# A second dense half, pairwise transposes of x, earlier weight loads and an explicit token order in an attention and MLP kernel

## The chip, the cores and the metric

The kernel runs on one core of one Trainium2 chip. The metric is the device time of one execution in microseconds (us). A timed execution is a little longer than the profiled span of the same run: 338.30 us beside a span of 336.5 us for the changed kernel. "x2", "y1" and the like are short names of experiments, which are told below. Where several executions were timed, medians are given. A ratio is the mean time of one kernel's fast runs over that of the other's fast runs of the same rounds, so it is not quite the ratio of the medians quoted. "Fast", "slow" and "unknown" are the states that each run was recorded with; a single look has the state "unknown".

## The reference

Block-sparse attention feeds a two-layer MLP with an exact GELU. Four batches, eight heads, 768 positions, 64 channels; blocks of 32 positions, so 24 blocks.

```python
mask = abs(blk_i - blk_j) <= 1
mask |= (blk_i == 0) | (blk_j == 0) | (blk_i == 23) | (blk_j == 23)
for qb in range(24):                        # three drawn key blocks for each query block
    for kb in sampled_blocks[qb]:
        mask[qb*32:qb*32+32, kb*32:kb*32+32] = True
attn = softmax(where(mask, q @ k.T / 8, -1e9)) @ v
x    = attn.transpose(0, 2, 1, 3).reshape(3072, 512)
out  = gelu(x @ w_in) @ w_out               # w_in 512 x 2048, w_out 2048 x 512
```

The first and the last block row attend to all keys. The text calls these the "dense rows".

## The kernel before

The work is cut into eight halves of 384 rows (two per batch), and a half goes through attention, the hidden layer and the output layer. The kernel overlaps the MLP of one half with the attention of the next. So a run has nine stages, which I bound by the first `hp` (hidden-layer) matmul of each half: an opening (attention of the first half alone), seven stages with the MLP of one half and the attention of the next, and a last one with an MLP alone.

Sparse attention gathers key blocks into `kg` and value blocks into `v_gat` with indirect copies on POOL. The first half of batch 0 instead computes all scores, with a one-hot matmul that adds -30000 to the barred blocks, and so needs no gathers:

```python
def first_scores(hp, t):                    # dense scores of a pair of heads, key tile t
    for l, r_, first_ in ((onehot..., barred..., True), (st["k", hp], st["q", hp], False)):
        for h in range(2): pe.matmul(s1[:, h, 0:HALF], lhsT=l[r, c], rhs=r_[r, 0:HALF], ...)
    act.activation(first_pt[hp % 3][:, t], s1[:, :, 0:HALF], AF.Exp, scale=scale)
```

A "record" is one DMA transfer as the profile lists it; the profile's views call it a packet. v goes through the queue of SP (sync). k, q and the weights go through the queue of POOL (gpsimd), but for the first k and q, which SP loads ahead of v. The weights wait until v has been cast: `after_values` touches w_in's tile on DVE after the casts, and the load must follow that write.

```python
first_v = load_v(0, sp)          # 6 loads of 256 KB, each record 64 floats = 256 B
...
for w in "kq": st["st", w, 1] = load_qk(0, w, 1)      # POOL's queue, records of 768 B written
...
def after_values():
    for n in range(NT): own_v(0, first_v, n, n + 1, dve)      # v_flat <- st_v, six casts
    for c in range(2):
        dve.memset(w_in_sb[:, 0:1, 1024 * c:1024 * c + 1], 0.0)
        load_w_in(c)                                   # POOL's queue
extra = {..., (2, 1): after_values and value_validity,
         (3, 1): first_weighted(1), load_w_out(0), load_w_out(1), four gathers of k, ...}
```

The other parts that the argument touches:

```python
mm_pool = tc.tile_pool(name="mm_pool", bufs=2, space=PSUM)  # op, psx, psd and ps share 2 buffers

def transpose_qk(b, hp, which, pair, eng, st):
    dst = qkt_pool.tile([P, S], BF16, tag=f"t{which}", ...)   # tk or tq
    ps = mm_pool.tile([P, NT, P], BF16, tag="mm", name="ps")
    ... 12 pe.transpose ...
    cast(eng, dst..., ps...)                                  # on DVE

def transpose_x(b, hb, m, st):          # after all four pairs: rows m of x, four transposes
    ps = mm_pool.tile([P, KIN, P], BF16, tag="mm", name="psx")
    ...
def place_xd(b, hb, st):                # dense rows into xT, just before the hidden layer
    dve.tensor_copy(st["xT", hb][:, :, c], st["xdT"][:, :, hb*BLOCK:hb*BLOCK+BLOCK])
```

The order of issue came from two helpers: `weave` put a given number of output steps between attention steps, and `spread` put the gathers and transposes for later evenly among the hidden steps.

The softmax here doesn't subtract the row's maximum and nothing guards it: scores larger than these inputs give would overflow.

Of the kernel before, what the change touches and what calls it, by code (L numbers as in the profile page):

```python
# [58 lines left out]
def weave(main, fill):  # L59

    fill = list(fill)
    for step, n in main:
        step()
        for f in fill[:n]:
            f()
        del fill[:n]
    for f in fill:
        f()


def spread(steps, aux):

    out, n, m = [], len(steps), len(aux)
    for i, step in enumerate(steps):
        out += aux[m * i // n:m * (i + 1) // n] + [step]
    return out
# [3 lines left out]
def kernel(  # L80
# [23 lines left out]
    kg_pool = ctx.enter_context(tc.tile_pool(name="kg_pool", bufs=4))  # L104
# [3 lines left out]
    first_ctx = ExitStack()  # L108
    first = first_ctx.enter_context(tc.tile_pool(name="first", bufs=1))
# [27 lines left out]

    sts = [dict() for _ in range(B)]
# [4 lines left out]
    for i, (w, x) in enumerate((("k", k), ("q", q))):  # L143
        t = w_out_sb.bitcast(F32)[:, 3 * i:3 * i + 3, :].rearrange("p a c -> p (a c)")
        first_st[w] = t.rearrange("p (h c) -> p h c", h=2)
        sp.dma_start(out=first_st[w], in_=x[0, 0:2].rearrange("h (p j) d -> p h (j d)", j=NT))
        if i == 0:
            sp.dma_start(out=raw,
                         in_=bass.AP(tensor=src, offset=0, ap=[[0, P], [1, NB * NR * 2]]))
# [31 lines left out]

    key_i = small("key_i", [1], I32)
    key_b = small("key_b", [1])
    onehot = small("onehot", [NB, BLOCK], BF16, first)
    seen = small("seen", [NB // 2])
# [3 lines left out]
    dve.tensor_scalar(onehot, blocks.unsqueeze(2).to_broadcast([P, NB, BLOCK]),  # L189
                      key_b[:, 0:1], None, op0=ALU.is_equal)  # L190
    dve.tensor_scalar(seen, blocks[:, 0:NB // 2], key_b[:, 0:1], None, op0=ALU.subtract)
# [5 lines left out]
    dve.memset(seen[:, 0:1], 1.0)  # L197

# [8 lines left out]
    for t in kgl[0] + qgl:  # L207
        dve.memset(t, 0.0)
    dve.memset(v_own[0][:, :, :, D:2 * GW], 1.0)

    sbi = small("sbi", [NB, NR], I32)
    sbf = small("sbf", [NB, NR])
    hit = small("hit", [NB // 2, NR])
    barred = small("barred", [NB // 2, BLOCK], BF16, first)
    dve.tensor_copy(sbi, raw[:, :, :, 0])
    dve.tensor_copy(sbf, sbi)
    dve.tensor_scalar(hit, sbf[:, 0:NB // 2, :], key_b[:, 0:1], None, op0=ALU.is_equal)
    for s in range(NR):
        dve.tensor_add(seen, seen, hit[:, :, s])
    dve.tensor_scalar(barred, seen.unsqueeze(2).to_broadcast([P, NB // 2, BLOCK]),  # L220
# [15 lines left out]
    iota(mask_ka, [[4, 4], [1, NR]], 0, 0)  # L236
    iota(rowm, [[4, 4]], 3, 0)
    iota(cols, [[4, 3]], 3, 0)
    iota(qbt, [[1, NQ], [0, NR]], 1, 0)
    pool.memset(base_v, float(NULL))  # L240
    iota(base_v[96:128, 3::4], [[1, 5]], 0, 0)
    iota(base_v[96:128, 2:19:4], [[1, 5]], 7, 0)
# [3 lines left out]
    for w in "kq":  # L246
        st["st", w, 1] = load_qk(0, w, 1)

# [165 lines left out]
    def gather_k(b, hb, hp, st):  # L414
        kg = kg_pool.tile([P, NQH, P], BF16, tag=f"kg{hb}", name=f"kg{hb}")
        st["kg", hb, hp] = kg
        pool.indirect_copy(
            kg.bitcast(F32).rearrange("p n (s c) -> p (n s) c", c=BLOCK // 2),
            st["k", hp].bitcast(F32).rearrange("p (n c) -> p n c", c=BLOCK // 2),
            idx_k[:, hb, 0:3], i_know_this_is_slow=True)  # L420


    def scores(b, hb, hp, st):
# [3 lines left out]
        pt = p_pool.tile([P, 2, 2, 512], BF16, tag="pt", name="pt")  # L427
# [44 lines left out]
    def weighted(b, hb, hp, st):  # L472
        pt, vo, gl = st["pt", hb, hp], v_own[b % 2], vgl[b % 2]
        x = st["x", hb]
# [18 lines left out]
        normalise(x[:, :, hp * P:hp * P + P].rearrange("p m (h d) -> p m h d", h=2), og, MH)  # L493
# [11 lines left out]
    first_pt = [first.tile([P, NT, 2, HALF], BF16, name="first_pt")]  # L505
    for t in v_gat:
        first_pt.append(t.rearrange("p n h e -> p (n h e)")[:, 0:NT * 2 * HALF]
                        .rearrange("p (t h c) -> p t h c", t=NT, h=2))

    def first_scores(hp, t):  # L510
        s1 = sc_pool.tile([P, 2, 512], F32, tag="sc", name="s1")
        c = slice(t * P, t * P + P)
        for l, r_, first_ in ((onehot.rearrange("p n c -> p (n c)"),
                               barred.rearrange("p n c -> p (n c)"), True),
                              (st["k", hp], st["q", hp], False)):
            for h in range(2):
                r = slice(64 * h, 64 * h + 64)
                pe.matmul(s1[:, h, 0:HALF], lhsT=l[r, c], rhs=r_[r, 0:HALF],
                          start=first_, stop=not first_)
        act.activation(first_pt[hp % 3][:, t], s1[:, :, 0:HALF], AF.Exp, scale=scale)  # L520

    def first_weighted(hp):
        og = og_pool.tile([P, MH, 2, VW], F32, tag="og", name="og")
        for m in range(MH):
            for h in range(2):
                for t in range(NT):
                    pe.matmul(og[:, m, h, :], lhsT=first_pt[hp % 3][:, t, h, m * P:m * P + P],
                              rhs=v_own[0][:, t, 2 * hp + h, 0:VW],
                              start=(m == h == t == 0), stop=True, skip_group_check=True)
        normalise(st["x", 0][:, :, hp * P:hp * P + P].rearrange("p m (h d) -> p m h d", h=2),  # L530
                  og, MH)

    def new_x(b, hb, st):
        st["x", hb] = x_pool.tile([P, MH, D_MODEL], BF16, tag="x", name="x")
        st["xT", hb] = x_pool.tile([P, KIN, HALF], BF16, tag="xT", name="xT")
        if hb == (b == 0):
            st["xd"] = x_pool.tile([P, NPAIR, P], BF16, tag="xd", name="xd")

    def transpose_x(b, hb, m, st):
        x, xT = st["x", hb], st["xT", hb]  # L540
        ps = mm_pool.tile([P, KIN, P], BF16, tag="mm", name="psx")
        for i in range(KIN):
            pe.transpose(ps[:, i, :], x[:, m, i * P:i * P + P], ident)
        lo, hi = (BLOCK if b > 0 and hb == m == 0 else 0), (P - BLOCK if hb == 1 and m == MH - 1 else P)
        dve.tensor_copy(xT[:, :, m * P + lo:m * P + hi], ps[:, :, lo:hi])
# [13 lines left out]

    def attention_steps(b, hb, st):  # L560

        new_x(b, hb, st)
        S_ = lambda hp: lambda: scores(b, hb, hp, st)
        W_ = lambda hp: lambda: weighted(b, hb, hp, st)
        D_ = lambda hp: lambda: dense_scores(hp, st)
        E_ = lambda hp: lambda: dense_weighted(b, hp, st)
        X_ = lambda m: lambda: transpose_x(b, hb, m, st)
        if hb == (b == 0):
            steps = [(S_(0), 3), (D_(0), 2)]
            for hp in range(1, NPAIR):  # L570
                steps += [(S_(hp), 0), (E_(hp - 1), 0), (W_(hp - 1), 2), (D_(hp), 2)]
            steps += [(E_(3), 0), (W_(3), 3), (lambda: transpose_xd(st), 0),
                      (X_(0), 0), (X_(1), 1), (X_(2), 0), (lambda: place_xd(b, hb, st), 0)]
        else:
            steps = [(S_(0), 5)]
            for hp in range(1, NPAIR):
                steps += [(S_(hp), 0), (W_(hp - 1), 4)]
            steps += [(W_(3), 3), (X_(0), 0), (X_(1), 1), (X_(2), 0),
                      (lambda: place_xd(b, hb, st), 0)]
        return steps  # L580

# [46 lines left out]
    def first_pair(hp):  # L628
        i = 2 * (hp % 2)
        for w in "kq":  # L630
            pair = st["st", w, hp // 2][:, i:i + 2, :]
# [3 lines left out]
        for w in "kq":  # L635
            globals_qk(0, hp, w, pool, st)

    def load_batch(b):
        st = sts[b]
        for n in range(2):  # L640
            for w in "kq":
                st["st", w, n] = load_qk(b, w, n)


    def after_values():
        for n in range(NT):
            own_v(0, first_v, n, n + 1, dve)
        for c in range(2):
            dve.memset(w_in_sb[:, 0:1, 1024 * c:1024 * c + 1], 0.0)
            load_w_in(c)  # L650

    def rotate_first():
        for r in range(1, 4):
            dve.memset(v_all[:, NT * r:NT * r + 1, 0:1, 0:1], 0.0)
            rotate_v(0, r, sp)

    new_x(0, 0, st)
    first_pair(0)
    extra = {(0, 3): lambda: first_pair(1),
             (1, 1): lambda: first_pair(2),  # L660
             (1, 3): lambda: first_pair(3),
             (2, 1): lambda: [after_values(), value_validity()],
             (2, 3): lambda: [first_weighted(0), gather_constants(), key_indices()],
             (3, 1): lambda: [first_weighted(1), load_w_out(0), load_w_out(1)]
             + [f() for f in k_steps(0, 1, range(NPAIR))],
             (3, 3): lambda: [first_weighted(2), rotate_first(), value_columns()]}
    for hp in range(NPAIR):
        for t in range(NT):
            first_scores(hp, t)
            extra.get((hp, t), lambda: None)()  # L670
    first_weighted(NPAIR - 1)
    for m in range(MH):
        transpose_x(0, 0, m, st)
    value_indices(0, dve)
    clear_mask()
    for i in range(2):
        clear_globals(i, dve)
    for i in range(2):
        mark_valid(i)
    first_ctx.close()  # L680
    g_pool = ctx.enter_context(tc.tile_pool(name="g_pool", bufs=1))
    os_pool = ctx.enter_context(tc.tile_pool(name="os_pool", bufs=2))

    value_indices(1, dve)
    sts[1]["st", "v"] = load_v(1, sp, dve)

    def transpose_step(b, hp):
        i = 2 * (hp % 2)
# [96 lines left out]
```

## Time and profile before

| | before |
|---|---|
| timed | 322.62 us (321.71 to 323.01, 4 runs) |
| span of the profiled run | 320.1 us |
| PE busy | 273.6 us, 85% |
| stages, us | 37.6, 44.1, 44.7, 32.2, 37.6, 32.2, 36.6, 30.4, 24.9 |
| v's last record begins | 19.8 us |
| w_in's load may begin | after the casts of v, which end at 23.0 us |

The prediction below read two boundaries by eye, 37.5 and 29.6; by one rule they are 36.6 and 30.4, with the same sum.

The page of the kernel before, its first two parts. The digits are tenths of busy share in 40 equal slices of 8 us; PEclk is the granted clock of the tensor engine in tenths.

```profile
span 320.1 us, 8104 instructions
PE 273.6 (85%) x3560; PEld 163.4 (51%) x3560; DVE 136.8 (43%) x366; ACT 156.1 (49%) x206; POOL 100.7 (31%) x149
...
PE   1778596698993998989997998989997989899995
...
PEclk9999899799996899999999999999999999999999
DMA  6949999999960049007791590009500000010001
```

PE is full from the middle on, so PE is what a change must relieve. The first third has holes, and the clock drops to 7, 6 and 8 there. The waits of PE in the same kernel (engine and tile, who released it; then us in total, number, longest) name the holes.

```profile
PE ps L54 <- ACT st L54: 7.7, 2, 4.8
PE s L54 <- POOL kg L54: 5.7, 2, 5.1
PE op L54 <- DMA w_out_sb<-in_moe_w_out_dram: 5.1, 2, 3.1
```

The first is the start of the kernel, the longest part of the second (5.1 us, up to 101.2 us, in stage 3) waits for the key gathers of batch 1, which stand on POOL behind that batch's value gathers (these from 88.71 us on, the first key gather from 99.95 to 101.14), and the third for w_out, which comes late because it stands behind the gate (POOL issues w_in at 23.3 us and w_out at 24.8).

From 51 to 57 us the second batch's v (q1, 256 B records) shared the DMA engines with w_out (q0, 1024 B records). The DMA view of that window gives packets, MB and a share of the engines:

```profile
q0 software_dynamic: 930, 0.94, 91.6%
q1 hardware_dynamic: 925, 0.24, 29.7%
```

The two queues moved the same number of records, and so very different numbers of bytes.

### The profile page before, as it was taken

To read this page: it belongs to the slowest core of one execution; us is meant where nothing else is said; L and a number is where in the kernel's file an instruction comes from. 1 tells how busy PE (TensorE), PEld (TensorE's weight loads), DVE (VectorE), ACT (ScalarE), POOL (GpSimd) and SP (SyncE) were. 2 spreads that over 40 slices of the span, in tenths; PEclk is the share of its full clock that TensorE was granted. 3 is DMA by queue.
4 is the path that set the end of the run, shared out by engine and by line. 5 is a ranking of instruction groups with operands and counts; after the bars stand their busy time and mean duration, and the time that the engine had idled before them with its cause. 6 is when DMAs were issued, how large, how long until landed. Compare 5 with 4: busy or idle time off the path is not lost. (4 is left out here: it accounts for less than half of the span.)

```text
span 320.1 us, 8104 instructions
## 1 busy us (share of the span) xinstructions
PE 273.6 (85%) x3560; PEld 163.4 (51%) x3560; DVE 136.8 (43%) x366; ACT 156.1 (49%) x206; POOL 100.7 (31%) x149
## 2 busy tenths in 40 slices
PE   1778596698993998989997998989997989899995
PEld 0345353464561654646564654646564645465642
DVE  5488871066460355415632555245440461035001
ACT  3587066254343660466256651576247634753620
POOL 6133422610054554343445554321244430000000
PEclk9999899799996899999999999999999999999999
DMA  6949999999960049007791590009500000010001
GB/s 156 205 94 167 216 234 199 191 209 237 250 132 0 20 76 173 35 0 175 198 202 29 69 199 33 2 2 240 167 2 2 35 35 33 2 35 35 33 35 66
DMA packets 42131, 33.79 MB, mean 106 GB/s; under 512 B 26096, under 2 KB 36464, under 8 KB 42096
## 3 DMA queue, kind: packets, MB, share of 16 engines
q1 hardware_dynamic: 31024, 23.18, 29.3%
q0 software_dynamic: 11072, 10.09, 20.2%
q8 instruction: 28, 0.46, 0.6%
q14 instruction: 7, 0.06, 0.1%
HBM read 27.34 MB, written 6.29 MB: 105 GB/s over the span
## 5 line engine op out<-in xcount | busy, mean ns | idle before, releaser
L54 PE MATMUL op<-w_out_sb,g 128*128 128x512 bf16 x384 | 97.3, 390 | 5.1 <-DMA w_out_sb<-in_moe_w_out_dram 5.1
L54 ACT ACTIVATE g<-hp 128x768 bf16<-128x768 f32 x64 | 51.7, 810 | 85.5 <-PE hp L54 85.5
L54 PE MATMUL hp<-xT,w_in_sb 128*128 128x384 bf16 x512 | 88.4, 331 | 1.9 <-DVE os L54 0.9
L54 PEld LDWEIGHTS <-w_in_sb 128*128 128x128 bf16 x512 | 49.5, 99 | 36.9 <-issue 4.4
L54 ACT ACTIVATE pt<-s 128x1024 bf16<-128x1024 f32 (+2 forms) x84 | 51.6, 687 | 26.1 <-PE s L54 13.3
L54 DVE TENSOR_TENSOR pt<-pt,mask_x 128x768 bf16<-128x768 bf16 x28 | 17.4, 620 | 96.6 <-ACT pt L54 96.4
L54 POOL INDIRECT_COPY v_gat<-v_flat,idx_v 128x1024 f32 (+1 forms) x21 | 33.4, 1592 | 78.4 <-issue 36.6
L54 POOL INDIRECT_COPY kg<-tk,idx_k 128x704 f32 x28 | 34.1, 1219 | 67.8 <-issue 58.1
L54 PEld LDWEIGHTS <-g 128*128 128x128 bf16 x384 | 34.5, 100 | 38.5 <-issue 8.3
L54 DVE COPY tk<-ps 128x768 bf16<-128x768 bf16 x16 | 15.3, 957 | 33.2 <-PE ps L54 33.2
L54 ACT ACT_TABLE_LOAD x16 | 20.5, 1283 | 17.9 <-PE s L54 9.3
L54 DVE COPY os<-op 128x512 f32<-128x512 f32 x24 | 16.6, 692 | 24.2 <-PE op L54 22.2
L54 PEld LDWEIGHTS <-tk 64*128 64x128 bf16 (+1 forms) x312 | 15.1, 98 | 20.2 <-issue 16.7
L54 PE MATMUL ps<-ident,st 128*64 128x128 bf16 x384 | 15.0, 229 | 8.0 <-ACT st L54 7.7
L54 PE MATMUL s<-tq,kg 64*128 64x32 bf16 x616 | 12.3, 174 | 10.8 <-POOL kg L54 5.7
L54 PEld LDWEIGHTS <-pt 128*32 128x32 bf16 (+1 forms) x868 | 19.8, 97 | 2.5 <-DVE x L54 0.3
L54 PE MATMUL s<-tq,tk 64*128 64x128 bf16 (+1 forms) x216 | 18.5, 252 | 1.3 <-ACT pt L54 0.7
L54 PEld LDWEIGHTS <-st 128*64 128x64 bf16 x384 | 12.0, 114 | 13.4 <-ACT st L54 7.9
L54 DVE TENSOR_TENSOR x<-og,rc 128x384 bf16<-128x384 f32 x32 | 17.8, 558 | 1.1
L54 ACT ACTIVATE pd<-sd 128x768 bf16<-128x768 f32 x16 | 13.0, 813 | 9.9 <-PE sd L54 9.9
L54 PEld LDWEIGHTS <-kg 64*128 64x128 bf16 x616 | 11.2, 94 | 12.5 <-issue 6.3
L54 PE MATMUL psx<-ident,x 128*128 128x128 bf16 x96 | 9.3, 219 | 9.0 <-DVE xT L54 3.7
(110 smaller groups left out, 233.2 us busy)
## 6 DMA issues: line engine op xcount, KB each, us to landing
st_v<-in_v_dram SPq DMA_DIRECT2D x24, 256.0 KB, 6.1
out_dram<-os SPq DMA_DIRECT2D x24, 256.0 KB, 3.1
v_flat<-v_flat SPq DMA_DIRECT2D x8, 594.0 KB, 7.3
v_flat<-v_flat SPq DMA_DIRECT2D x8, 396.0 KB, 5.5
st<-in_k_dram POOLq DMA_DIRECT2D x7, 384.0 KB, 7.2
st<-in_q_dram POOLq DMA_DIRECT2D x7, 384.0 KB, 10.3
w_in_sb<-in_moe_w_in_dram POOLq DMA_DIRECT2D x2, 1024.0 KB, 13.1
w_out_sb<-in_moe_w_out_dram POOLq DMA_DIRECT2D x2, 1024.0 KB, 32.3
```

The costliest lines, as they stand in the source:

```text
L54: return self._tc.keep_in_program_order(f(*args, **kwargs))
```

## The change

The intent: (a) let the second half of batch 0 attend densely too, so that batch 0 needs no gathers and no rotation of its v; (b) transpose x pair by pair, as soon as a pair is normalised; (c) replace the two ordering helpers by strings of tokens, one for each phase, which say exactly what is issued when; and (d) issue the weights' loads at once, without the gate. The core of the diff, cuts marked by "...":

```diff
-def weave(main, fill): ...
-def spread(steps, aux): ...
+OPENING = """
+A0 P0 P1 F00 F01 F02 F03 A1 F04 F05 F10 F11 F12 A2 F13 F14 F15 J0 J1 J2 J3 J4 J5 F20 F21 V0 F22 A3 F23 X0 F24 F25
+F30 V1 F31 F32 X1 F33 V2 F34 F35 X2 V3 X3 N L1"""
+FIRST = """
+H I0 H I1 H M1 I2 H H I3 H I4 H I5 H
+O2 F00 F01 O2 F02 F03 O2 F04 F05 O1 I6 F10 F11 V0 F12 F13 X0 O2 I7 F14 F15 O2 F20 F21 V1 F22 F23 B R X1 O2 I8
+F24 F25 T0 K00 O2 F30 F31 V2 F32 F33 X2 O2 T1 K01 F34 F35 O2 V3 Q0 Q1 O2 X3 O3"""
+SECOND = """
+H H T2 K02 C00 C01 C02 H H T3 K03 G H H H M2 H
+..."""
+SPARSE = """
+H H H H H H H H
+O2 S0 O6 B R W0 S1 O3 X0 T0 K00 W1 S2 O3 X1 T1 K01 W2 S3 O4 X2 C00 C01 C02 W3 O4 X3 Z O2"""
+...
     for w in "kq":
         st["st", w, 1] = load_qk(0, w, 1)
+    for c in range(2):
+        load_w_in(c)
...
-    def first_scores(hp, t):
+    def first_scores(hb, hp, t):
...
-    def transpose_x(b, hb, m, st):
-        x, xT = st["x", hb], st["xT", hb]
-        ps = mm_pool.tile([P, KIN, P], BF16, tag="mm", name="psx")
-        for i in range(KIN):
-            pe.transpose(ps[:, i, :], x[:, m, i * P:i * P + P], ident)
+    def transpose_x(b, hb, hp, st):
+        x, xT = st["x", hb, hp], st["xT", hb]
+        ps = og_pool.tile([P, MH, P], BF16, tag="og", name="psx")
+        for m in range(MH):
+            pe.transpose(ps[:, m, :], x[:, m, :], ident)
...
-    def after_values():
-        for n in range(NT):
-            own_v(0, first_v, n, n + 1, dve)
-        for c in range(2):
-            dve.memset(w_in_sb[:, 0:1, 1024 * c:1024 * c + 1], 0.0)
-            load_w_in(c)
-
-    def rotate_first(): ...
```

The tokens that the text uses: H is two tiles of the hidden layer, O2 two output steps, F dense scores, V a dense weighted sum, J a cast of v, T the transposes of k and q of a pair, K and C gathers of keys and values, X a transpose of x, Z the placing of dense rows, P the load of half of w_out, L1 the loads of k and q of batch 1.

## The prediction

> **What bounds it now.** The tensor engine: the first table gives PE 273.6 of 320.1 us, and the chain of waits that ends last is PE work (`op`, `hp`). In the time-ordered view of PE, from one stage's first `hp` matmul to the next: opening 37.6 us, then 44.1, 44.7, 32.2, 37.6, 32.2, 37.5, 29.6, 24.7. Starts of back-to-back matmuls give: hidden layer 10.4, output 10.4, a sparse pair 1.46, dense rows of a pair 0.68, a pair's transposes 0.80, a dense-mask half 7.9 + 4.8. So a half with dense rows needs 31.8, a sparse one 28.9. The rest is waits (waits of PE): 5.1 us for `kg` (gap at 96 us), 5.1 for `w_out_sb`, 7.7 for `st`, short ones for `xT`, `xdT`, `pt`; and the clock fell to 0.66 to 0.76 around 35 to 65 us.
>
> **Removed.** For batch 0: the rotation of v (384 records of 6336 B, about 420 ns each over 16 engines: 10 us of DMA), four `kg` and three `v_gat` gathers (3.3 and 3.7 us start to start on POOL), 8.5 us of PE, and the index chain before its first gathers.
>
> **Added.** A second dense-mask half: 24 exponentials (0.72 us apart, 17.5 us ACT) and 12.7 us PE among output matmuls; two scores and two output steps cost PE 1.52 us and ACT about 1.5: PE-bound.
>
> **Moved.** xT pair by pair removes 1 to 1.5 us of transpose waits per half; two output steps before the first scores hide 0.6 us behind the last gelu. But transposes of k and q now lie in sparse output phases, where an output accumulator holds one of two PSUM buffers: about 1.1 us lost each (one `tk` copy, 0.96). Batch 1's first value gathers follow `kg` 2: about 3 us wait for `v_gat` in the third stage.
>
> **The catch.** Before, the w_in load waited behind the casts of v. Now w_in and w_out are queued right behind k and q. [...]while w_out and the next v shared the engines, 149 and 155 packets began in one us. v is 6144 packets of 256 B. I estimate 2750 have gone when k and q finish (14 us); 3400 then pair with 1024 w_in packets (91 a us, estimated from 102 alone) and 2048 of w_out (152 a us beside v, measured). So v lands near 39 us, not 19.5. The first weighted sum needs all of it[...]: PE idles from about 22 to 39 us.
>
> **Sum (estimate).** Weighted sum begins 39.5; rest of opening 13; stages 38.5, 36, 31.5, 33.8, 31.5, 33.8, 28.3, 24.7: span 310.6. Timed runs are 2.8 above the profiled span: **313 us**, 8 in 10 within 297 to 323. Chances: faster 0.60, same 0.36, slower 0.04.
>
> **Right if:** the page shows PE idle for 15 us or more before the first `og`, v's last landing at 37 to 42 us, no wait for `w_out_sb`, no 5 us `kg` gap, hidden phases of 10.4 us at full clock, later stages of about 34 and 31.5 us.
>
> **Wrong if:** v isn't starved: about 297. Or DVE, with 14 us of index work in the second stage, or POOL's gathers hold PE longer: 320 or more. Or the transpose stalls in sparse halves are absent: 4 us less.

The sum: 39.5 + 13 + 38.5 + 36 + 31.5 + 33.8 + 31.5 + 33.8 + 28.3 + 24.7 = 310.6. That records of two queues pair one for one rests on the trace of before alone (149 and 155 in one us), and that PE stands still until all of v is there was my estimate; the changed kernel's trace shows it below (13 matmuls in 25.6 us).

## More of the kernel before

The stage lengths are worked out from the times of the matmul records (first `hp` of a stage to the next; the last runs to the end of the span).

In the time-ordered view of PE (start, duration) the first weighted sum runs through without a pause:

```profile
23.64 1.26 PE L54 MATMUL og<-v_flat,first_pt 128*128 128x65 bf16 x36
```

## The result, and the profile after

The change made the kernel slower.

| | before | after |
|---|---|---|
| timed, median | 322.62 us (321.71 to 323.01, 4 runs) | 338.31 us (338.19 to 340.24, 4 runs) |
| ratio to before, 95% | 1 | 1.051 (1.048 to 1.054) |
| profiled span | 320.1 us | 336.5 us |

By stage, in us:

| stage | 1 (opening) | 2 | 3 | 4 | 5 | 6 | 7 | 8 | 9 |
|---|---|---|---|---|---|---|---|---|---|
| attention in it | batch 0, first half | batch 0, second half | 1, dense rows | 1 | 2, dense rows | 2 | 3, dense rows | 3 | none |
| before | 37.6 | 44.1 | 44.7 | 32.2 | 37.6 | 32.2 | 36.6 | 30.4 | 24.9 |
| predicted | 52.5 | 38.5 | 36.0 | 31.5 | 33.8 | 31.5 | 33.8 | 28.3 | 24.7 |
| after | 62.8 | 47.0 | 37.8 | 34.6 | 33.6 | 34.5 | 33.3 | 28.2 | 24.8 |

The opening lost 25.2 us. The other stages together gained 8.8 us of span.

The page after, the same parts, and the first entries of its chain that ended last (share of the span by tile):

```profile
span 336.5 us, 7970 instructions
PE 274.3 (82%) x3500; PEld 165.0 (49%) x3500; DVE 141.4 (42%) x351; ACT 163.3 (49%) x214; POOL 86.4 (26%) x126
...
PE   0850039898978998979887999998879999999995
...
PEclk9995559999979997999999999999999999999998
DMA  6999956090092820930393949102920011000001
...
PE hp L54 22%; PE op L54 18%; DMA st_v<-in_v_dram 8%; PE og L54 8%; SPq L54 7%; PE s L54 7%; PE ps L54 3%; DVE xT L54 3%; DVE v_flat L54 2%; DVE tk L54 2%; DVE pt_all L54 2%; PE psx L54 2%; ACT v_gat L54 1%; POOL v_gat L54 1%; PE od L54 1%
```

PE's row has a hole from the third slice to the sixth, in which the clock drops to half, while DMA stays at 9 for most of it. The chain that ended last now runs through the load of v (`st_v`, 8%). PE's waits after:

```profile
PE og L54 <- DVE v_flat L54: 23.9, 4, 6.6
PE ps L54 <- ACT st L54: 8.3, 2, 8.1
PE ps L54 <- DVE tk L54: 7.8, 6, 2.6
PE hp L54 <- DVE os L54: 4.1, 2, 2.0
PE s L54 <- ACT kg_all L54: 3.3, 10, 1.0
PE hp L54 <- DVE xT L54: 2.6, 2, 1.9
```

The waits for `kg` and for `w_out_sb` are gone, as intended. In their place stand 23.9 us for `v_flat`, the casts of v. (`kg_all` in the line of ACT isn't a gather: its space holds dense exponentials in the opening.) The time-ordered view of PE after, around the first weighted sum, shows the four pieces of that wait:

```profile
23.27 0.24 PE L54 MATMUL og<-v_flat,kg_all 128*128 128x65 bf16 x2
29.00 0.21 PE L54 MATMUL og<-v_flat,kg_all 128*128 128x65 bf16 x1 [5.49 <-DVE v_flat L54]
35.81 0.21 PE L54 MATMUL og<-v_flat,kg_all 128*128 128x65 bf16 x1 [6.60 <-DVE v_flat L54]
42.58 0.21 PE L54 MATMUL og<-v_flat,kg_all 128*128 128x65 bf16 x1 [6.55 <-DVE v_flat L54]
48.02 1.87 PE L54 MATMUL og<-v_flat,kg_all 128*128 128x65 bf16 x31 [5.22 <-DVE v_flat L54]
```

Each of the first matmuls needs one more of v's six chunks, and the chunks come 5.4 to 6.8 us apart. The view of the tile `st_v` (the landing buffer of v), first 60 us, says that DVE's casts waited for the loads and not for anything of their own, and PE for the casts:

```profile
  DMA st_v<-in_v_dram: 24.0, 4
...
  DVE v_flat L54: 24.0, 4
  PE og L54: 23.9, 4
```

The view by windows of 22.4 to 48.0 us (length, then busy time and number of PE, PEld, DVE, ACT and POOL, granted clock, DMA share, GB/s) confirms that hardly anything but DMA worked:

```profile
22.40:48.00 25.60, 1.55 (x13) 0.57 (x9) 1.71 (x4) 1.79 (x3) 0.00 (x0) 0.53 1.10 178
```

And why v was slow: the DMA view of 17 to 27 us (w_in on q0 against v on q1), as packets, MB and share, and after it that of 29 to 39 us (w_out on q0 against v).

```profile
q0 software_dynamic: 923, 1.80, 94.9%
q1 hardware_dynamic: 920, 0.23, 17.7%
```

```profile
q0 software_dynamic: 1547, 1.57, 92.0%
q1 hardware_dynamic: 1547, 0.39, 29.7%
```

The two queues start equal numbers of records, so they take turns record by record. A record of w_in holds 2048 B and one of v 256 B, so v got an eighth of the weights' bytes while w_in was moving, and a quarter while w_out was.

### The profile page after: what moved, and what is told of

Same layout as the page of the kernel before. It is cut to its first block, busy times and chain, and to the rows that moved or that the text cites. A ratio compares the mean times of both kernels' runs of the same rounds, so it can differ in the third digit from the quotient of the medians.

```text
span 336.5 us, 7970 instructions
## 1 busy us (share of the span) xinstructions
PE 274.3 (82%) x3500; PEld 165.0 (49%) x3500; DVE 141.4 (42%) x351; ACT 163.3 (49%) x214; POOL 86.4 (26%) x126
## 4 chain that ended last, share of the span: by engine, by line
PE 62%; DVE 11%; DMA 8%; SPq 7%; issue 5%; ACT 4%; POOL 2%; DVEq 0%; ACTq 0%
PE hp L54 22%; PE op L54 18%; DMA st_v<-in_v_dram 8%; PE og L54 8%; SPq L54 7%; PE s L54 7%; PE ps L54 3%; DVE xT L54 3%; DVE v_flat L54 2%; DVE tk L54 2%; DVE pt_all L54 2%; PE psx L54 2%; ACT v_gat L54 1%; POOL v_gat L54 1%; PE od L54 1%
## 5 line engine op out<-in xcount | busy, mean ns | idle before, releaser
L54 ACT ACTIVATE pt_all<-s 128x1024 bf16<-128x1024 f32 (+2 forms) x72 | 44.2, 687 | 36.3 <-PE s L54 36.2
L54 DVE TENSOR_TENSOR pt_all<-pt_all,mask_x 128x768 bf16<-128x768 bf16 x24 | 17.3, 721 | 66.7 <-ACT pt_all L54 66.7
L54 POOL INDIRECT_COPY kg_all<-tk,idx_k 128x704 f32 x24 | 28.5, 1189 | 53.9 <-issue 46.9
L54 ACT ACTIVATE v_gat<-s 128x768 bf16<-128x768 f32 x24 | 18.0, 809 | 39.1 <-PE s L54 39.1
L54 PE MATMUL s<-tq,tk 64*128 64x128 bf16 (+1 forms) x240 | 25.9, 276 | 4.9 <-ACT kg_all L54 3.3
L54 PEld LDWEIGHTS <-kg_all 64*128 64x128 bf16 (+1 forms) x672 | 15.3, 97 | 25.9 <-issue 25.9
L54 PEld LDWEIGHTS <-pt_all 128*32 128x32 bf16 (+2 forms) x840 | 22.1, 97 | 10.4 <-issue 2.0
L54 PE MATMUL og<-v_flat,kg_all 128*128 128x65 bf16 x144 | 7.2, 214 | 23.9 <-DVE v_flat L54 23.9
L54 PEld LDWEIGHTS <-tk 64*128 64x128 bf16 (+1 forms) x312 | 15.8, 97 | 22.0 <-issue 14.8
L54 DVE COPY tk<-ps 128x768 bf16<-128x768 bf16 x16 | 15.3, 957 | 26.4 <-PE ps L54 25.9
L54 ACT ACT_TABLE_LOAD x16 | 20.5, 1283 | 7.0 <-PE hp L54 5.1
L54 POOL COPY kgl<-tk 64x64 bf16<-64x64 bf16 x24 | 5.6, 235 | 68.0 <-DVE tk L54 67.5
L54 ACT ACTIVATE kg_all<-s 128x768 bf16<-128x768 f32 x24 | 17.9, 809 | 6.7 <-PE s L54 6.7
```

Source lines behind the costliest of these rows:

```text
L54: return self._tc.keep_in_program_order(f(*args, **kwargs))
```

## The experiments

The theory after reading the trace was: **the opening is lost to the order of loads, v being starved record by record, and nothing else there matters.** Its rivals: the second dense half or the longer first exponentials made the opening long; or bytes, not records, are what the queues share; or the early weights fill some general DMA limit whatever queue they use. For the later stages, two smaller theories: the transposes T among output steps stall PE on a PSUM buffer; and the placing copy (Z) collides with POOL's gathers. Twelve kernels were run, all correct.

Where one kernel builds on another the text says so. A kernel timed in rounds has a median; the others were run once, with their state unknown, and are read for their traces. Of the kernel before, each call of the chip had its own runs, with medians from 321.5 to 322.2 us.

### Gate the weights behind v again: x1_gated

Edit, against the changed kernel:

```diff
-A0 P0 P1 F00 ... J4 J5 F20 F21 V0 ...
+A0 F00 ... J4 J5 U P0 P1 F20 F21 V0 ...          # U: touch w_in after the casts, then load it
-    for c in range(2):
-        load_w_in(c)
```

> The changed kernel with one thing put back: both w_in loads wait for the casts of batch 0's v, and the w_out loads follow them in the queue. Theory (v is starved by weight packets that take turns with it): v lands near 20 us instead of 47, the first weighted sum runs at about 23 us instead of 48, PE has no gap of 5 us or more after 10 us; span falls by about 25 us to 312, timed 313 to 315. Rival (the opening is late because of the new token order or the second dense half): the gap goes but the time comes back later, span above 325.

Measured: 313.39 us (312.46 to 313.91, 4 runs), ratio to before 0.977 (0.973 to 0.981), which at 2% counts as unclear; span 310.7. The opening fell from 62.8 to 36.5 us; every later stage stayed within 0.4 us of the changed kernel's. v's last record began at 20.5 us. In PE's time-ordered view the first weighted sum is whole again:

```profile
22.85 1.51 PE L54 MATMUL og<-v_flat,kg_all 128*128 128x65 bf16 x36
```

So the order of loads costs 25.8 us of span (336.5 less 310.7), more than the whole loss. The rest of the change is worth a gain of 9.4 us of span over before (320.1 less 310.7).

### Put v ahead of the weights in their own queue: x2_v_on_pool_queue

No gate: the queue and the order of v's loads change, and nothing in the program waits for v. As the trace shows below, the size of v's records changes with the queue.

```diff
-    first_v = load_v(0, sp)
...
     for w in "kq":
         st["st", w, 1] = load_qk(0, w, 1)
+    first_v = load_v(0, pool)
     for c in range(2):
         load_w_in(c)
```

> The changed kernel with batch 0's v issued on the gpsimd queue, behind k and q and ahead of the weights: same bytes, same start, nothing waits. Theory (two queues take turns packet by packet[...]): v lands at 20 to 22 us, first weighted sum near 23 us, weights all in by 42 us, span 310 to 313. Rival (the DMA engines are simply full, 13 MB have to come in before the first 45 us are over): v still lands after 35 us and the span stays within 3 us of 336.

Measured: 311.61 us (310.70 to 313.61, 4 runs), ratio 0.973 (0.968 to 0.978); span 308.9; opening 36.7 us. The casts of v ended at 23.36 us (changed kernel: 47.96). The DMA view of 8 to 26 us names one data queue alone:

```profile
q0 software_dynamic: 2390, 3.94, 113.7%
```

"The early weights fill DMA whatever the queue" falls: the weights came in about as early (the last records of w_in and w_out began at 30.7 and 40.9 us, in the changed kernel at 28.6 and 42.0), and PE waited no more for v.

The run changes more than the order, though. In the trace's DMA records v went through POOL's queue as 384 records of 4096 B, where SP's queue had 6144 of 256 B. And POOL issued the two loads of w_in at 12.2 and 14.2 us, after v's, instead of from 4.6 us on. So x2 doesn't say how much of the cure is order and how much the larger records. x1 shows that order alone is enough: there v still has records of 256 B, and the opening is 36.5 us.

### Halve the weights' records: x3_half_packets

```diff
-        f = slice(1024 * c, 1024 * c + 1024)
-        pool.dma_start(out=w_in_sb[:, :, f], in_=w_in_v[:, :, f])
+        for a in range(1024 * c, 1024 * c + 1024, 512):
+            pool.dma_start(out=w_in_sb[:, :, a:a + 512], in_=w_in_v[:, :, a:a + 512])
```

and w_out's 512 columns in two loads of 256 likewise: the same bytes in records of half the size.

> The changed kernel with the weights loaded in rows of half the length: the same bytes and order, twice as many packets. Theory (turns are by packet, not by byte): v gets about twice the turns per weight byte, all of it in at about 40 us instead of 47, first weighted sum 7 us earlier than 48, span about 330. Rival (share by bytes): half-size packets change nothing for v or[...] make it later; span 336 or more.

Measured, one look: 329.15 us, span 327.4; opening 55.2 us; v's last record at 38.6 instead of 47.1 us. The DMA view of 17 to 27 us:

```profile
q0 software_dynamic: 1559, 1.55, 91.1%
q1 hardware_dynamic: 1561, 0.39, 29.9%
```

The counts are still equal, and v's share of the bytes doubled, from an eighth to a quarter of w_in's. Sharing by bytes would have left v's bytes as they were. It is record for record.

### The early weights alone, in the kernel before: x4_before_ungated

```diff
     for w in "kq":
         st["st", w, 1] = load_qk(0, w, 1)
+    for c in range(2):
+        load_w_in(c)
...
-        for c in range(2):
-            dve.memset(w_in_sb[:, 0:1, 1024 * c:1024 * c + 1], 0.0)
-            load_w_in(c)
...
     first_pair(0)
+    load_w_out(0)
+    load_w_out(1)
```

> The kernel before with only this part of the change: w_in and w_out queued right behind k and q, no wait for v. Theory: v lands near 41 us, first weighted sum waits until then (23.6 before), PE gap of about 17 us; part comes back because the waits for w_out (5 us) and the slow clock of the second stage go; span about 328 to 332. Rival (earlier weights help, what hurts in the changed kernel is its new order): span 320 or less.

Measured, one look: 334.43 us, span 332.6. The opening is 59.0 us (37.6 before), though nothing else of the change is there; v's last record begins at 42.3 us. Stage 2 falls from 44.1 to 36.3 us; of that, the wait of 5.1 us for `w_out_sb` is gone from the list of PE's waits. From PE's waits:

```profile
PE og L54 <- DVE v_flat L54: 19.2, 3, 7.2
```

The token order and the second dense half are not needed for the loss.

### The next batch's loads, held back: z1_next_loads_later

The prediction had left one thing out. The first loads of batch 1's k and q (L1) are issued at 15 to 17 us, since all that POOL waits for there is a free buffer (2.96 us for PE, which reads it), and so stand in the queue behind w_out; the last of v then takes turns with them (from 42 to 44 us 390 records began on q0 and 375 on q1). This edit makes those loads wait for a DVE write that comes after the casts of v.

```diff
+        if behind:
+            dve.memset(t[:, :, 0:1], 0.0)      # only for batch 1
         pool.dma_start(out=t, in_=src[b, ...])
```

> The changed kernel with batch 1's first loads of k and q held behind the opening's vector work, so that only the weights share the engines with batch 0's v. Theory (v's last packets, 530 of 6144 when w_out is done at 42 us, then took turns with batch 1's k and q until 47 us): v is all in at 42 to 43 us, the rest of the first weighted sum starts at 43 to 44 us instead of 48.0; span about 332. Rival (v was late for another reason, its own queue): 47 to 48 us again, span 336.

Measured, one look: 334.32 us, span 332.6 (336.5); v's last record at 42.9 us (47.1); opening 58.7 (62.8); the rest as in the changed kernel. The term left out is 4.2 us.

### Where the remaining gain comes from: y4_before_v_on_pool_queue

The edit is x4 with v's six loads moved onto POOL's queue ahead of w_in, as in x2. It gives the kernel before the good load order (with v in records of 4096 B, as in x2) and nothing else of the change.

> The kernel before with the weights queued early and batch 0's v ahead of them on the same gpsimd queue; no second dense half, no new order. Theory (nearly all that x2_v_on_pool_queue gained over the kernel before comes from weights that arrive early): opening 37 to 38 us, stage 2 about 36.5 as in x4_before_ungated instead of 44.1, the rest as before; span 309 to 312, timed 311 to 315, so within 3 us of x2_v_on_pool_queue. Rival (the second dense half and the token order carry the gain): timed 318 or more.

Measured: 317.15 us (316.98 to 318.64, 4 runs), ratio 0.988 (0.982 to 0.994); span 315.0. It lies between the theory's 311 to 315 and the rival's 318 or more. So the load order, done well, is worth 5.1 us of the 11.2 us of span that x2 gains over before, and the second dense half with its token order 6.1 (315.0 less 308.9). By stage, x2 less this kernel: -2.5, +7.8, -7.3, +2.4, -2.8, +2.4, -3.5, -2.2, -0.1. By the medians the same split is 4.6 of 10.0 us. The change as written gains in dense-row stages (3, 5, 7) and gives back in stages 2, 4 and 6. In stage 3 the gain holds the wait for batch 1's key gathers, which is still 5.4 us in this kernel and gone in x2. The next experiments look at why.

### The placing copy on another engine: y1_place_on_act

In the changed kernel, stage 3 ends with PE waiting 1.9 us for `xT`, and stages 4 and 6 end with waits of 2.0 us each. The view puts those two down to `os`, an output copy that DVE does right behind the placing copy; both end at the same time (250.25 and 250.26 us in stage 6). The time-ordered view of DVE, changed kernel, at the end of stage 6, and after it that of POOL at the same place:

```profile
247.70 2.56 DVE L54 COPY xT<-xdT 128x128 bf16<-128x128 bf16 x1
```

```profile
248.56 1.65 POOL L54 INDIRECT_COPY v_gat<-v_flat,idx_v 128x1024 f32 x1 [2.00 <-PE op L54]
```

A small copy took 2.56 us and ended at 250.26; the gather's record ends at 250.21, though it began 0.86 us after the copy's. The other slow ones agree: the copy ended at 147.57, 182.12 and 283.52 us, gathers at 147.49, 182.07 and 283.48. The view of the tile `xT` gives the copy's spread (number, then min, median and max ns), first of the changed kernel:

```profile
L54 DVE COPY xT<-psx x32: 330/342/358, 53.2 to 311.2; 128x352 bf16<-128x352 bf16 x24, 128x384 bf16<-128x384 bf16 x8
L54 DVE COPY xT<-xdT x6: 184/1618/2561, 145.3 to 311.5; 128x128 bf16<-128x128 bf16 x6
```

The copies from PSUM (`psx`) never stretch, though four of them ran while a gather's record was open (332 to 358 ns); those within SBUF (`xdT`) do, up to 2.56 us. In the changed kernel the ends of the slow copies and of the gathers agree within 0.1 us; elsewhere the fit is looser (in x2 one copy ended 0.31 us after its gather's record, in z2 one 0.82 us after). What couples the two isn't shown by any run here. The test is to give the copy to another engine, ACT, on top of x2:

```diff
-        dve.tensor_copy(st["xT", hb][:, :, c], st["xdT"][...])
+        act.copy(st["xT", hb][:, :, c], st["xdT"][...])
```

> The kernel of x2_v_on_pool_queue with one thing changed: the copy that places the dense rows into xT runs on the scalar engine instead of the vector engine, at the same place in the order. Theory (that copy is held up[...]): the copy takes 0.5 us or less although the gather runs beside it, the 2 us waits of the hidden layer at the end of stages 3, 4 and 6 go; those stages fall from 37.8, 34.6, 34.6 to about 35.8, 32.6, 32.6; span 303 to 304 instead of 308.9. Rival (the strided 128x128 copy itself is slow): it stays at 2 us or more on the scalar engine, span stays within 1 us of 308.9.

Measured: 304.94 us (302.54 to 307.11, 4 runs, one of them slow and left out of the ratio), ratio to before 0.944 (0.936 to 0.951), where x2 had 0.973; span 303.9. The same view of this kernel:

```profile
L54 ACT COPY xT<-xdT x6: 298/304/310, 118.8 to 276.5; 128x128 bf16<-128x128 bf16 x6
```

Stage 3 went from 37.8 to 35.9 us, stages 4 and 6 from 34.6 to 32.5, and PE's waits of `hp` for `xT` and `os` are gone. In this kernel the copy ran some 3 us earlier in stages 4 and 6 than in x2, though, and no gather's record lies beside any of the six, so y1 alone doesn't show that a gather leaves ACT's copy alone. y8's trace does: a copy on ACT began at 236.60 us, inside a gather's record (236.12 to 237.56 us), and took 0.30 us.

### The gathers, moved after the copy in the token order: y2_gather_after_place

On top of x2, a different attack on the same collision: write the value gathers behind Z.

```diff
-... W2 S3 O4 X2 C00 C01 C02 W3 O4 X3 Z O2
+... W2 S3 O4 X2 W3 O4 X3 Z C00 C01 C02 O2
```

> The kernel of x2_v_on_pool_queue with the three value gathers of the sparse stages issued after the place copy instead of before it; the copy stays on the vector engine. Theory[...]: in stages 4 and 6 the copy falls from 2.5 us to 0.5 or less and those stages from 34.6 to about 32.6; stage 3, where the order is untouched, keeps its 2.2 us copy and its 37.8; span about 305. Rival (the copy itself is slow): no change of the copy's time.

Measured, one look: 310.58 us, span 308.8 (x2: 308.9); no stage moved by more than 0.1 us. The run is inconclusive about the collision, because the edit changed nothing on the chip: POOL's own order of instructions is the same in both, and the placing copy took 185 ns at least, 1781 in the median and 2680 at most, against 185, 1803 and 2698 in x2. The token further back in the program delayed nothing here.

### The gathers, made to wait: z2_gather_waits_for_place

On top of y2, a one-column POOL copy that reads the placed rows, so that the gathers behind it on POOL start after Z is done (at the end of stage 6 Z ended at 222.62 us, the POOL copy began at 222.69 and the next gather at 225.01).

```diff
+        if hb == 1 and b < B - 1:
+            pool.tensor_copy(wait_pool, st["xT", hb][:, 0, HALF - 1:HALF])
```

> y2 mended: there gpsimd's own order was not touched by the edit, so the gathers started as early as before. Here a one-element gpsimd copy reads what the place copy wrote in stages 4 and 6, so that the value gathers start after it; the copy stays on the vector engine. Theory[...]: the copy takes 0.2 to 0.5 us instead of 2.6, the hidden layer's 2 us wait goes, stages 4 and 6 fall from 34.6 to about 32.6; stage 3 keeps its 2.7 us copy; span about 305, less whatever later gathers cost. Rival (the copy is slow by itself): 2 us or more.

Measured, one look: 311.22 us, span 309.4. The placing copy at the end of stage 6, undisturbed, in DVE's time-ordered view (that of stage 4 took 0.18 us too):

```profile
222.44 0.18 DVE L54 COPY xT<-xdT 128x128 bf16<-128x128 bf16 x1
```

Stage 4 fell from 34.5 to 32.3 us, so the collision is the cause of that wait. Stage 6 lost the wait too, but fell only from 34.6 to 34.0 us, at a granted clock of 0.95 instead of 1.00. And stage 5 rose from 33.7 to 36.9, where the later gathers met another placing copy (3.35 us at most), and the total stayed. That a gather beside the copy stretches it is shown; the way it does so isn't. The gain was given back.

### The transposes of k and q, split in two: y3_split_transposes

The changed kernel's 7.8 us of `ps` waiting for `tk` come from T, in which the transposes of k and then of q follow at once. An output accumulator holds one of the two PSUM buffers, so q's transposes must wait until DVE has copied k's out. In stage 2 the wait is 2.55 us, since other DVE work is queued ahead of that copy (casts and index work from 89.61 us on; the copy begins at 93.71). The time-ordered view of PE, changed kernel:

```profile
91.64 0.53 PE L54 MATMUL ps<-ident,st 128*64 128x128 bf16 x12
94.71 0.53 PE L54 MATMUL ps<-ident,st 128*64 128x128 bf16 x12 [2.55 <-DVE tk L54]
```

On top of x2, T now transposes k alone and a new token U transposes q, with a few matmul groups between them:

```diff
-... X0 T0 K00 W1 S2 O3 X1 T1 K01 W2 S3 O4 ...
+... X0 T0 W1 S2 U0 K00 O3 X1 T1 W2 S3 U1 K01 O4 ...
```

> The kernel of x2_v_on_pool_queue with each pair's k and q transposes split, other matmuls between them, in stages 2, 4 and 6. Theory (an open output accumulator leaves one of two PSUM buffers, so q's transposes wait for the copy of k's): the waits of PE for tk fall from 7.8 us to under 2.5; stages 4 and 6 fall by about 2 us each from 34.6, stage 2 by 2 to 3 from 45.5; span about 302 to 303. Rival (the time is only moved, ScalarE or the vector engine sets the pace of these stages): span above 307.

Measured: 308.26 us (306.39 to 310.86, 4 runs), ratio 0.957 (0.949 to 0.964), where x2 had 0.973 (0.968 to 0.978); span 309.1, where 302 to 303 was expected. The profiled run is the slowest of its four (spans 309.1, 304.8, 308.2, 304.6; granted clock 0.983), and x2's was its fastest (clock 1.000), so these two spans say little. By the medians the split gained 3.4 us, about half of what was expected. The waits for `tk` fell as expected, but new ones came for `tq`:

```profile
PE hp L54 <- DVE xT L54: 6.8, 5, 2.4
...
PE op L54 <- DVE tq L54: 2.2, 2, 1.1
PE ps L54 <- DVE tk L54: 2.0, 1, 2.0
```

Now the output accumulator waits for the buffer that q's transposes hold. The waits of `hp` aren't new: the placing copy still collides, and x2 has 7.5 us there under `xT` and `os` together. Splitting alone moves part of the wait; the buffer has to be free.

### Transposes where no accumulator is open: y7_transposes_at_boundaries

On top of y1 (the placing copy on ACT): T and U are split as in y3, and put where an output tile of eight steps has just been finished, so that T takes the buffer of the one that was freed.

```diff
-O2 S0 O6 B R W0 S1 O3 X0 T0 K00 W1 S2 O3 X1 T1 K01 W2 S3 O4 X2 ...
+O2 S0 O6 T0 W0 S1 U0 K00 B R O3 X0 W1 S2 O3 X1 O2 T1 W2 S3 U1 K01 O2 X2 ...
```

Stage 2's string got the same treatment, with T0 ahead of the long casts and the index work on DVE.

> The kernel of y1_place_on_act with k and q transposes split, as in y3_split_transposes, but placed just after an output accumulator is finished (after 8 and 16 of the 24 output steps) instead of while one is open. Theory (y3 only turned the wait round: with both transposes in flight the next accumulator waited for its PSUM buffer): waits of PE for tk and tq in stages 2, 4 and 6 fall to under 2 us together, stage 2 from 45.5 to 47 down to 42 to 43, stages 4 and 6 from 32.5 to 30.5 to 31; span 295 to 297, timed about 298. Rival (the pace of these stages is set by ScalarE or the vector engine): span 302 or more.

Measured: 296.07 us (295.00 to 299.54, 6 runs), ratio 0.918 (0.916 to 0.921). The profiled run is slow, so its stage lengths are read with care: stage 2 went from 47.0 to 40.9 us (some 1.5 us of that is the clock, as told below) and stages 4 and 6 from 32.5 to 30.8, which the next kernel's fast run repeats. Of all waits for `tk` and `tq`, one of 1.1 us is left.

### Value gathers of batch 1 first: y8_gathers_first

On top of y7, the last wait that the prediction had named: `v_gat` in stage 3.

```diff
-H H T2 U2 K02 C00 C01 C02 H H T3 U3 K03 G H H H M2 H
+C00 C01 C02 H H T2 U2 K02 H H T3 U3 K03 G H H H M2 H
```

> The kernel of y7 with the three value gathers of stage 3 put before its kg gather of pair 2. Theory (W0 waits for the last value gather, 1.6 us[...]): that wait goes, stage 3 falls from 35.9 to about 34.3; timed 1.5 us below y7, about 296. Rival (a later kg gather then makes the scores of pair 2 or 3 wait): stage 3 stays within 0.5 us.

Measured: 294.30 us (291.98 to 295.64, 6 runs), ratio to before 0.914 (0.910 to 0.917). Its interval overlaps y7's, so the time alone doesn't separate the two. In stage 3 the wait of 1.5 us for `v_gat` is gone. The stage fell by more, from 35.9 us (y7 and y1) to 32.5 where 34.3 was expected; the other 1.9 us is PE's busy time, at a granted clock of 0.95 in y7 and 1.00 here. The stages are 36.3, 40.9, 32.5, 30.8, 32.3, 30.8, 33.3, 28.6, 24.7. Its page:

```profile
span 290.2 us, 7973 instructions
PE 268.0 (92%) x3500; PEld 161.2 (56%) x3500; DVE 130.1 (45%) x345; ACT 164.8 (57%) x220; POOL 94.0 (32%) x132
...
PE   0779798999999999999999999999999899999994
...
PEclk9999999999999999999999999999999999999999
```

PE is busy for 92% of the span and the clock is full throughout. This version beats the kernel before by 8.6% and, by the medians, the changed kernel by 13% (294.3 against 338.3). It has the whole change in it, plus five edits: v's queue and order, one copy's engine, the split of T, its places, and the place of three gathers.

## Why the prediction was wrong, and where it was right

It foresaw the starving of v, named it as the catch and put a number on it; but it made that number, and the later stages, too small, and so got the sign of the result wrong (313 us predicted with 0.04 for slower; 338.3 measured). In spans: 310.6 predicted, 336.5 measured, 25.9 us apart. The stages account for it: opening +10.3, stage 2 +8.5, stage 3 +1.8, stages 4 and 6 +3.1 and +3.0, the others together -0.7.

**The step that failed first: "So v lands near 39 us, not 19.5."** The mechanism was right, and shown by x1, x2, x3 and x4; the size was off. v's last record began at 47.1 us and PE resumed at 48.0 instead of 39.5, 8.5 of the 10.3 us. Two terms of the sum were wrong.
- "I estimate 2750 have gone when k and q finish (14 us)": by 14 us the trace after has 1961 records of v. The trace of before, which lay open, has 2395 at that time and could have been counted. The 789 records too many, at the rate of 152 in a us that the prediction used, are about 5.2 us (an estimate). Why v came more slowly than before in these 14 us (1961 against 2395) isn't shown.
- L1, the loads of batch 1, was missing from the list of what v would take turns with. z1 measures it at 4.2 us.
The two together give 9.4 us against the 8.5 seen; as z1's last record of v began at 42.9 us, the first term is rather 3.9 (42.9 less 39). The pairing rates were right within a few per cent: 92 records in a us beside w_in (predicted 91), 155 beside w_out (predicted 152), from the counts of the two windows. The last 1.8 us are the rest of the opening, 14.8 us instead of 13, in a window whose granted clock was 0.88.

**Second failed step: "stages 38.5, 36, 31.5, ..." — stage 2 took 47.0 us.** The sum had PE's work and none of its waits in that stage. The 2.55 us at T0 is one. Moving the transposes brought the stage from 45.5 (x2) to 40.9 (y7, y8), so 4.6 us belong to where T, U and the gather behind them stand (in x2, 3.9 of them are waits of `ps`). Another 1.5 us is the clock: after that gap the changed kernel ran at a granted 0.60 from 95 to 99 us, x2 at 1.00 after the same gap, and its stage took 45.5. The clock was lowest, 0.50, from 96.4 to 98.0 us; over the long gap of the opening, 22.4 to 48.0 us, it was 0.53. The 2.55 us gap cost the clock in one profile and not in the other; what decided between the two isn't shown. The remaining 2.4 us (40.9 less 38.5) I didn't test; it stays open.

**Third failed step: 31.5 for the sparse stages.** They took 34.6 and 34.5 us. The transposes' waits of 1.05 us each were foreseen. The placing copy was not: it takes up to 2.56 us beside POOL's gathers, next to which the new order put it, and PE waits for it (2.0 us in each of these stages in the changed kernel). y1 and z2 show it; the last 1.0 us (32.5 in y1 less 31.5) stays open. The same copy cost stage 3 1.9 us, which explains its 37.8 instead of 36.0 (35.9 in y1); that the wait for `v_gat` there was 1.5 us shorter than predicted hides a further miss there, at a granted clock of 0.95. Before had the same collision (the copy took 1.74 us in stage 5), a hint that the trace gave and I didn't use.

**What was right.** The mechanism of the catch; PE idle for more than 15 us around the first `og`; hidden phases of 10.4 to 10.5 us at full clock. No wait for `w_out_sb` was left, and no 5 us gap for `kg`. A `v_gat` wait came in stage 3, but 1.5 us of PE instead of 3. Stages 5, 7, 8 and 9 were right within 0.5 us; no run took their terms apart, so how much of that is luck isn't shown. "Wrong if v isn't starved: about 297" said what the change could be worth without its flaw; x2 measured 311.6, because the waits in stages 2, 4 and 6 remained, and only y7 and y8, which take those away as well, reach 296 and 294.

## What to carry to other kernels

Asking for a bulk load at the earliest moment wasn't free here, where a small-record load on another queue was still under way (PE waited 23.9 us): count records, not bytes (923 of 2048 B went beside 920 of 256 B), list everything that is in the queues at that time, and let what is needed first go first, by a gate (x1, opening 36.5 us instead of 62.8) or ahead in the same queue (x2, 36.7). Look at the records again after a change of queue, since their size can change with it (v's from 256 to 4096 B in x2). A rearranged program order need not change the time between engines (y2 moved the span by 0.1 us); look at which copies and gathers (2.56 us for a copy beside a gather, 0.18 without), and which holders of a shared PSUM buffer (waits of 1.05 to 2.55 us), it brings together. A sum of stages needs the waits of each stage as well as its work, and the old trace often shows them at a smaller size.

## Costs that these traces measured

- A load in 256 B records on SP's queue beside one in 2048 B records on POOL's got an eighth of its bytes (0.23 MB against 1.80 MB in 10 us); ahead in POOL's queue, in records of 4096 B, it brought the opening from 62.8 to 36.7 us.
- An indirect copy, from one start to the next where they follow at once: about 3.3 us for keys and mostly 3.0 to 3.7 us for values, with records of about 1.19 us for keys and 1.65 us for values of 128x1024.
- Transposes that share two PSUM buffers with an open accumulator: a wait of 1.05 us for each pair of heads, 2.55 us where DVE was busy.
